# Retention and a swish MLP on one core: where outputs of three chunks lie in PSUM, how the first weights are loaded and used, and the order of the second batch's steps

## The chip, the core and the metric

The kernel runs on one core of one Trainium2 chip. The metric is the device time of one execution in microseconds (us). TensorE is called PE below, VectorE DVE, ScalarE ACT, GpSimd POOL, and SyncE, which issues nearly all transfers, SP. Every engine works through its own list of instructions in a fixed order, and an instruction that waits holds up all that stand behind it on its engine.

## The reference

Inputs are q, k and v of 8 batches, 8 heads, 576 positions and 64 columns, and the weights of an MLP (512 to 2048 and back). All are float32.

```python
scores = scale * np.matmul(q, k.transpose(0, 1, 3, 2))
gamma = 1.0 - 2.0 ** (-5.0 - np.arange(H))
Dmat = np.where(rel >= 0, gamma[:, None, None] ** rel, 0.0)   # rel = row - column
attn = np.matmul(scores * Dmat, v)
x = attn.transpose(0, 2, 1, 3).reshape(B * S, H * D)          # 4608 x 512
h = x @ w_in
out = (h * (1.0 / (1.0 + np.exp(-beta * h)))) @ w_out
```

So there is a causal retention with a decay for each head, and then an MLP with a swish in it. The kernel folds the decay into q and k/v (`gq`, `gv`), so that the mask on the scores is a plain causal one.

## The kernel before

**Attention in chunks.** Of each batch the first 512 positions are four chunks of 128 keys. `seq` lists them: indices 0 to 3 are batch 0, 4 to 7 batch 1, and so on. For index i the steps are: `pre` (POOL casts the keys to `kn` and scales the values to `vn`), `t_k` (four PE transposes into PSUM, ACT copies them to `kT`), `a_sc` (16 PE matmuls make the scores of 8 heads in two PSUM tiles `sc`, DVE multiplies each by the mask into `R`, 128x512 at a time), `a_cross` (4 matmuls with the running state `sbd` of the chunks before), `a_O` (8 matmuls of `R` and `vn` into the output tile `O`), `a_x` (a copy of `O` to `xT`, the input of the MLP, on ACT or DVE), and `a_st` (4 matmuls that add to the state in PSUM, and two ACT copies of it to `sbd`, or to `end` after the last chunk). `t_q` transposes the queries.

**MLP in blocks of 512 rows.** `up(m, fo)` makes one of 16 slices of 128 hidden units: four matmuls over `ko` with 512 columns into a PSUM tile `ph`, and an ACT Silu into `gT`. `down(m, ms, f0)` is four matmuls into `po`; after 16 of them DVE copies `po` to `ot` and SP issues the store. The tiles `ph` and `po`, and some of attention, share the PSUM tag `mm` with three buffers, so a new `ph` waits until the third tile before it has been read. The tags `sc` and `O` have two buffers each; with `st` that makes eight banks. The steps of batch 1 do not all stay with their tag: `a_sc` of an odd index takes its two score tiles from `O`, and `t_k` of indices 6 and 7 transposes into `sc`.

**Order.** The first batch's attention is written out step by step, before any `up`. All that follows is one list `fill` of ups and downs, and `merged` puts further steps into it: each step has a number, and is issued ahead of the first entry of `fill` whose place is not below that number. Place `d0` is the first down of block 0, and `u1 = d0 + 16` the first up of block 1. There are 16 ups before `d0`.

**Weights.** SP loads `w_in` in pieces of columns (four of 256, then two of 512), each with all four `ko`, and behind them `w_out` in four parts of 1 MB, into staging tiles `wt` of 1 MB with four buffers. DVE and POOL cast the pieces to bfloat16 (`cast_w_in`). `cast_w_out` multiplies by 1/beta, three quarters on DVE and one on ACT; its first call stands at `d0 - 4`, so its ACT instruction lies between the Silus of hidden slices 11 and 12.

All of batch 1's loads come behind `w_out` on SP's queue.

Of the kernel before, what the change touches and what calls it, by code (L numbers as in the profile page):

```python
# [19 lines left out]
def kernel(  # L20
# [10 lines left out]
    nc = tc.nc  # L31
    B, H, S, D = q.shape
# [98 lines left out]
    for h in range(H):  # L131
# [16 lines left out]
    causal4 = consts.tile([P, HP, P], BF16, name="causal4")  # L148
    nc.gpsimd.tensor_copy(causal4[:], causal[:].unsqueeze(1).to_broadcast([P, HP, P]))

    causal2 = consts.tile([P, P], BF16, name="causal2")

    NS = 3
# [10 lines left out]
    tiny = consts.tile([P, FO], F32, name="tiny")  # L164
    WG = 4

    pieces = [(f, 256) for f in range(0, 1024, 256)] + [(f, 512) for f in range(1024, d_ff, 512)]
    NP = len(pieces)
    w_in_r = moe_w_in.rearrange("(ko ki) f -> ki ko f", ki=P)
    w_out_r = moe_w_out.rearrange("(fo fi) n -> fi fo n", fi=P)  # L170
# [2 lines left out]
    def load_w_in(g):  # L173
        f0, fn = pieces[g]
        if f0 % 512 == 0:
            whole[0] = stage.tile([P, KO, 512], F32, name="wt", tag="wt", bufs=4)
        t = whole[0][:, :, f0 % 512:f0 % 512 + fn]
        nc.sync.dma_start(t, w_in_r[:, :, f0:f0 + fn])  # L178
        wts[g] = t

    def cast_w_in(g, kos=range(KO)):
        t = wts[g]
        f0, fn = pieces[g]
        for ko in kos:
            on_pool = ko == KO - 1 or g < 4 and ko > 1
            (nc.gpsimd if on_pool else nc.vector).tensor_copy(w_in_sb[:, ko, f0:f0 + fn], t[:, ko])  # L186

    def load_w_out(g):
# [111 lines left out]
    def t_k(i):  # L300
        T = psum.tile([P, HP, P], BF16, name="T", tag="sc" if i in (CB + 2, CB + 3) else "O", bufs=2)
        for p in range(HP):
            nc.tensor.transpose(T[:, p, :], heads(live[i]["kn"], p), ident[:])  # L303
        nc.scalar.copy(live[i]["kT"], T[:])  # L304

    def q_cols(i, r, p):

        b, c = seq[i]
        if b is None:
            return live[i]["qkT"][r, 0, p, :], lambda o: o  # L310
        return (batch[b]["qT"][r, :, p, c * PC:(c + 1) * PC], lambda o: o.rearrange("k (i s) -> k i s", i=CB))

    def a_sc(i):
        L = live[i]
        L["R"] = R = sb.tile([P, 2, HP, P], BF16, name="R", tag="R", bufs=4)

        tag = "mm" if i == CB - 1 else "O" if i >= E and (i - E) % 2 else "sc"
        sc = [psum.tile([P, HP, P], F32, name="sc", tag=tag, bufs=3 if tag == "mm" else 2) for _ in range(2)]
        for p in range(HP):
            for j in range(2):  # L320
                r = slice(j * D, (j + 1) * D)
                rhs, view = q_cols(i, r, p)
                nc.tensor.matmul(view(sc[j][:, p, :]), L["kT"][r, p, :], rhs, start=True, stop=True,  # L323
                                 skip_group_check=True)
        mask = causal if seq[i][0] is not None else causal2
        m_b = mask[:].unsqueeze(1).to_broadcast([P, HP, P])
        if i == CB - 1:

            half = sb.tile([P, HP, P], BF16, name="half", tag="half", bufs=1)
            nc.scalar.copy(half[:], sc[1][:])  # L330
            sc[1] = half
        for j in range(2):
            nc.vector.tensor_tensor(R[:, j], sc[j][:], causal4[:] if i == CB - 1 else m_b, ALU.mult)  # L333

    def a_cross(i, first):

        b, c = seq[i]
        L = live[i]
        if first:
            L["O"] = psum.tile([P, HP, P], F32, name="O", tag="O", bufs=2)  # L340
        if c == 0 and b is not None:
            return
        for p in range(HP):
            rhs, view = q_cols(i, slice(0, P), p)
            if b is None:
                for x in range(2):
                    r = slice(x * TL, (x + 1) * TL)
                    nc.tensor.matmul(L["O"][:, p, r], ends[(2 * c + x) % 4][:, p, :], rhs[:, r],
                                     start=False, stop=True, skip_group_check=True)
            else:  # L350
                nc.tensor.matmul(view(L["O"][:, p, :]), sbds[(c - 1) % NS][:, p, :], rhs,  # L351
                                 start=first and p == 0, stop=not first, skip_group_check=True)

    def a_O(i):

        b, c = seq[i]
        L = live[i]

        early = i < E
        if not early:  # L360
            tag = "sc" if b is not None and b >= QB and c > 1 else "O"
            L["O"] = psum.tile([P, HP, P], F32, name="O", tag=tag, bufs=2)
        O, R, vn = L["O"], L["R"], L["vn"]
        crossed = b is None or c > 0
        for j, p in [(n // HP, n % HP) if early else (n % 2, n // 2) for n in range(H)]:
            nc.tensor.matmul(O[j * D:(j + 1) * D, p, :], vn[:, 2 * p + j, :], R[:, j, p, :],  # L366
                             start=p == 0 and not (early and crossed), stop=early or not crossed,
                             skip_group_check=True)
        if early:
            a_x(i)  # L370

    def a_x(i):
        b, c = seq[i]
        O = live[i]["O"]
        if b is None:
            x = xt(B)[:, :, c, :]
        else:
            x, O = xt(b)[:, :, :, c * PC:(c + 1) * PC], O.rearrange("k p (i s) -> k p i s", i=CB)
        if i == CB - 1:
            nc.vector.tensor_copy(x[:, :2], O[:, :2])  # L380
            nc.scalar.copy(x[:, 2:], O[:, 2:])
        else:
            on_act = i < E or i % 2 == 0 if i < 2 * E else b is not None and c == 1
            (nc.scalar.copy if on_act else nc.vector.tensor_copy)(x, O[:])  # L384
# [21 lines left out]
    def up(m, fo, c0=0, cn=CB):  # L406
        if m not in gts:
            gts[m] = sb.tile([P, FO, CB, P], BF16, name="gT", tag="gT", bufs=2)
        w = slice(c0 * PC, (c0 + cn) * PC)
        ph = psum.tile([P, CB, P], F32, name="ph", tag="mm", bufs=3)  # L410
        ph = ph.rearrange("f i s -> f (i s)")[:, :cn * P].rearrange("f (i s) -> f i s", i=CB)
        for ko in range(KO):
            nc.tensor.matmul(ph, w_in_sb[:, ko, fo * P:(fo + 1) * P], xts[m][:, ko, :, w],  # L413
                             start=(ko == 0), stop=(ko == KO - 1))
        nc.scalar.activation(gts[m][:, fo, :, w], ph, ACT.Silu, scale=beta_sb[:, fo:fo + 1])  # L415
# [37 lines left out]
    def F(f, *a):  # L453
        return lambda: f(*a)
# [26 lines left out]
    pre(3, (0,))  # L481
    a_sc(2)
    t_k(3)
    warm_up(1, 128)
    a_cross(2, True)
    a_sc(3)
    pre(2, (1,))
    a_st(2)
    a_O(2)
    pre(3, (1,))  # L490
    warm_up(2, 128)
    a_cross(3, True)
    a_O(3)
    cast_w_in(0)
    a_st(3)
    cast_w_in(1)
# [4 lines left out]
                            fill=0.0, base=0, channel_multiplier=-1)  # L501
    nc.gpsimd.memset(causal2[:TL, TL:], 0.0)

    fill = [F(up, 0, fo) for fo in range(FO)]
    d0 = len(fill)
    fill += [F(down, 0, ms, f0) for f0 in range(0, FO, 4) for ms in range(3)]
    fill += [F(down, 0, 3, f0) for f0 in range(0, FO, 4)]
# [13 lines left out]
    def second(i):  # L521
        for f in (a_O, lambda j: a_cross(j, False), a_x):
# [98 lines left out]
```

## Time and profile before

| | us |
|---|---|
| median of three runs (311.30 to 312.04) | 311.78 |
| the profiled execution, in all | 311.92 |
| its span, first to last instruction | 310.1 |
| PE busy in the span | 298.5 (96%) |
| ACT busy | 143.0 (46%) |
| DVE busy | 106.9 (34%) |
| POOL busy | 96.0 (31%) |

The profiled execution is 0.14 us above the median, and 1.8 us of it lie outside the span. The granted TensorE clock is 0.998 of full speed over the whole span. A matmul of 512 columns starts 0.216 us after the one before it when nothing waits, one of 256 columns 0.108 us, one of 128 columns 0.056 us; the longer means in the profile's groups (365 ns for the 512 columns) count the pipeline's depth too. Some matmul records are missing from the trace; such a hole looks like an idle PE of 0.2 us with the reason "issue".

### The profile page before, as it was taken

How to read it: one execution, taken by the hardware profiler on the slowest of the kernel's cores; microseconds unless marked ns; L12 is line 12 of the kernel's file. 1: busy time of each engine (PE TensorE's matmuls, PEld its weight loads, DVE VectorE, ACT ScalarE, POOL GpSimd, SP SyncE). 2: the span in 40 equal slices, each digit the busy share in tenths (PEclk: the TensorE clock that was granted, in tenths of full speed). 3: DMA queues.
4: the chain of work that ended last, by engine and by line, in shares of the span. 5: the costliest groups of instructions: out<-in, count | busy, mean ns of one | idle time of the engine just before them, and what ended most of it. 6: DMA issues, size and time to landing. Idle time of an engine off the chain costs nothing.

```text
span 310.1 us, 5363 instructions
## 1 busy us (share of the span) xinstructions
PE 298.5 (96%) x2144; PEld 157.8 (51%) x2177; DVE 106.9 (34%) x191; ACT 143.0 (46%) x256; POOL 96.0 (31%) x131
## 2 busy tenths in 40 slices
PE   7789999999999999999999999999999999999995
PEld 5544456775544454454554545455545444444444
DVE  7554476342531342434430434043405420010012
ACT  5567626995138412560186117711673037207700
POOL 4663026846524282254308031902420000000000
PEclk9999999999999999999999999999999999999999
DMA  8999999998989999999897697968852110031011
GB/s 207 221 355 387 380 232 273 233 257 179 202 197 162 224 189 235 218 212 198 133 234 107 136 205 207 201 115 192 196 76 37 68 70 0 17 88 34 0 70 68
DMA packets 123897, 52.79 MB, mean 170 GB/s; under 512 B 105680, under 2 KB 116320, under 8 KB 123872
## 3 DMA queue, kind: packets, MB, share of 16 engines
q1 hardware_dynamic: 98496, 46.15, 61.5%
q10 hardware_dynamic: 25376, 6.30, 13.6%
q8 instruction: 17, 0.28, 0.4%
q14 instruction: 8, 0.07, 0.1%
HBM read 36.71 MB, written 9.44 MB: 149 GB/s over the span
## 4 chain that ended last, share of the span: by engine, by line
PE 85%; DMA 6%; SPq 5%; DVE 1%; issue 1%; ACT 1%; POOL 1%; POOLq 0%
PE po L426 40%; PE ph L413 35%; DMA wt<-in_moe_w_in_dram 4%; SPq L94 3%; PE O L366 3%; PE sc L323 3%; DMA qn<-in_q_dram 2%; PE O L351 2%; PE st L396 2%; SPq L178 1%; POOL qs L247 1%; PE T L297 1%; PE T L303 1%; ACT gT L415 0%; DVE xT L384 0%
## 5 line engine op out<-in xcount | busy, mean ns | idle before, releaser
L415 ACT ACTIVATE gT<-ph,beta_sb 128x512 bf16<-128x512 f32 (+1 forms) x154 | 99.2, 659 | 86.3 <-PE ph L413 83.4
L413 PE MATMUL ph<-xT,w_in_sb 128*128 128x512 bf16 (+1 forms) x600 | 129.3, 365 | 3.2 <-DVE w_in_sb L186 0.9
L426 PE MATMUL po<-w_out_sb,gT 128*128 128x512 bf16 (+2 forms) x591 | 126.7, 368 | 1.1 <-issue 0.3
L413 PEld LDWEIGHTS <-w_in_sb 128*128 128x128 bf16 x616 | 58.7, 98 | 65.0 <-DVE w_in_sb L186 2.3
L426 PEld LDWEIGHTS <-gT 128*128 128x128 bf16 x608 | 57.1, 98 | 62.5
L333 DVE TENSOR_TENSOR R<-sc,causal 128x512 bf16<-128x512 f32 x71 | 44.3, 684 | 68.9 <-PE sc L323 68.9
L433 DVE COPY ot<-po 128x512 f32<-128x512 f32 (+2 forms) x38 | 25.0, 662 | 92.1 <-PE po L426 92.0
L255 POOL TENSOR_TENSOR vn<-kvn,gv 128x512 bf16<-128x512 f32 x32 | 33.4, 1042 | 22.8 <-DMA kvn<-in_v_dram 11.5
L247 POOL TENSOR_TENSOR qs<-qn,gq 128x512 bf16<-128x512 f32 x24 | 24.3, 1042 | 33.2 <-DMA qn<-in_q_dram 33.2
L273 POOL CAST kn<-kvn 128x512 bf16<-128x512 f32 x32 | 19.6, 612 | 47.7 <-DMA kvn<-in_k_dram 47.3
L401 ACT CAST sbd<-st 64x256 bf16<-64x256 f32 x48 | 17.4, 362 | 15.0 <-PE st L396 14.3
L384 DVE CAST xT<-O 128x512 bf16<-128x512 f32 x24 | 15.8, 688 | 19.6 <-PE O L366 9.6
L384 ACT CAST xT<-O 128x512 bf16<-128x512 f32 x11 | 6.4, 586 | 32.2 <-PE O L351 25.2
L396 PE MATMUL st<-vn,kn 128*128 128x128 bf16 x128 | 12.4, 219 | 0.2 <-POOL vn L255 0.2
L396 PEld LDWEIGHTS <-kn 128*128 128x128 bf16 x128 | 9.3, 98 | 5.0 <-issue 0.2
L366 PE MATMUL O<-R,vn 128*64 128x128 bf16 x288 | 10.7, 221 | 0.0
L323 PE MATMUL sc<-qT,kT 64*128 64x128 bf16 x256 | 10.3, 217 | 0.4 <-ACT kT L304 0.2
L366 PEld LDWEIGHTS <-vn 128*64 128x64 bf16 x288 | 8.5, 110 | 4.1 <-issue 3.6
L323 PEld LDWEIGHTS <-kT 64*128 64x128 bf16 x288 | 8.1, 94 | 3.8 <-ACT kT L304 1.5
L304 ACT COPY kT<-T 128x512 bf16<-128x512 bf16 x12 | 6.9, 586 | 4.8 <-PE T L303 4.8
L208 PE MATMUL ph<-warm 128*128 128x128 f32 (+1 forms) x24 | 7.0, 429 | 1.2 <-DVE warm L119 1.2
L186 DVE CAST w_in_sb<-wt 128x256 bf16<-128x256 f32 (+1 forms) x14 | 6.0, 476 | 5.2 <-DMA wt<-in_moe_w_in_dram 5.2
(56 smaller groups left out, 90.2 us busy)
## 6 DMA issues: line engine op xcount, KB each, us to landing
qn<-in_q_dram SPq DMA_DIRECT2D x16, 512.0 KB, 5.8
kvn<-in_k_dram SPq DMA_DIRECT2D x32, 256.0 KB, 5.9
kvn<-in_v_dram SPq DMA_DIRECT2D x32, 256.0 KB, 5.6
out_dram<-ot SPq DMA_DIRECT2D x31, 256.0 KB, 2.7
wt<-in_moe_w_out_dram SPq DMA_DIRECT2D x4, 1024.0 KB, 9.5
wt<-in_moe_w_in_dram SPq DMA_DIRECT2D x4, 512.0 KB, 7.5
wt<-in_moe_w_in_dram SPq DMA_DIRECT2D x2, 1024.0 KB, 11.8
out_dram<-ot SPq DMA_DIRECT2D x9, 128.0 KB, 2.4
```

The costliest lines, as they stand in the source:

```text
L247: e.tensor_tensor(batch[b]["qs"][:, cs, hs], q_tiles[b][:, hs, cs].rearrange("p h i d -> p i h d"), gq[:, cs, hs].unsqueeze(3).to_broadcas ...
L255: nc.gpsimd.tensor_tensor(live[i]["vn"][:], kv_tiles.pop(i)[:, 1], gains(gv, c), ALU.mult)
L273: nc.gpsimd.tensor_copy(kn[:, c % 2], t[:, 0])
L323: nc.tensor.matmul(view(sc[j][:, p, :]), L["kT"][r, p, :], rhs, start=True, stop=True, skip_group_check=True)
L333: nc.vector.tensor_tensor(R[:, j], sc[j][:], causal4[:] if i == CB - 1 else m_b, ALU.mult)
L366: nc.tensor.matmul(O[j * D:(j + 1) * D, p, :], vn[:, 2 * p + j, :], R[:, j, p, :], start=p == 0 and not (early and crossed), stop=early or ...
L384: (nc.scalar.copy if on_act else nc.vector.tensor_copy)(x, O[:])
L396: nc.tensor.matmul(st[:, p, :], heads(L["kn"], p), heads(L["vn"], p), start=(c == 0 and p == 0), stop=True, skip_group_check=True)
L413: nc.tensor.matmul(ph, w_in_sb[:, ko, fo * P:(fo + 1) * P], xts[m][:, ko, :, w], start=(ko == 0), stop=(ko == KO - 1))
L415: nc.scalar.activation(gts[m][:, fo, :, w], ph, ACT.Silu, scale=beta_sb[:, fo:fo + 1])
L426: nc.tensor.matmul(po[:, :nn], gT[:, fo, ms, :], w_out_sb[:, fo, n0:n0 + nn], start=(fo == 0), stop=(fo == FO - 1))
L433: nc.vector.tensor_copy(ot, po[:, :nn])
```

## The change

It has five parts, which all act in the first 70 us of the program or so.

- The output tiles of indices 3, 5 and 7 are made as two tiles of half the width in two PSUM banks (`split`), and `a_x` copies one on DVE and the other on ACT. Before, index 3 was one bank copied by both engines in turn, and 5 and 7 were one bank copied by DVE.
- The mask of index 3 no longer goes through an ACT copy (`half`) and a widened mask (`causal4`); DVE reads both score tiles from PSUM. The last copies and the third `a_cross` of batch 0 change places with other steps.
- `w_in` is loaded in six pieces of 256 columns and one of 512; the first two are loaded in two halves each, `ko` 0 and 1 and then 2 and 3. `up_pair` makes hidden slices 0 and 1, and then 2 and 3, two at a time: both with `ko` 0 and 1 first, then both with 2 and 3. POOL now casts every second `ko` (`ko` 0 and 1 of the first piece).
- Steps of batch 1 are moved: `t_q` 0 by one place, `t_k` 5 by one, both `a_sc` of indices 4 and 5 by one, `a_st` 4 by one, `t_k` 6 behind `second(4)`, `t_k` 7 by one, and `a_sc` and `a_st` of 6 and 7 by one to two.
- `a_x` of batch 0 becomes a step of its own.

```diff
-    pieces = [(f, 256) for f in range(0, 1024, 256)] + [(f, 512) for f in range(1024, d_ff, 512)]
+    pieces = [(f, 256) for f in range(0, 1536, 256)] + [(f, 512) for f in range(1536, d_ff, 512)]
...
-        nc.sync.dma_start(t, w_in_r[:, :, f0:f0 + fn])
+        for w in (slice(0, 2), slice(2, KO)) if g < 2 else (slice(0, KO),):
+            nc.sync.dma_start(t[:, w], w_in_r[:, w, f0:f0 + fn])
...
-            on_pool = ko == KO - 1 or g < 4 and ko > 1
+            on_pool = ko < 2 if g == 0 else ko % 2
...
-        if i == CB - 1:
-            half = sb.tile([P, HP, P], BF16, name="half", tag="half", bufs=1)
-            nc.scalar.copy(half[:], sc[1][:])
-            sc[1] = half
         for j in range(2):
-            nc.vector.tensor_tensor(R[:, j], sc[j][:], causal4[:] if i == CB - 1 else m_b, ALU.mult)
+            nc.vector.tensor_tensor(R[:, j], sc[j][:], m_b, ALU.mult)
+    def split(i):
+        return i in (CB - 1, CB + 1, 2 * CB - 1)
+    def new_O(i):
+        b, c = seq[i]
+        if split(i):
+            tags = ("sc", "sc") if i == CB - 1 else ("O", "sc")
+            live[i]["O"] = [psum.tile([P, 2, P], F32, name="O", tag=t, bufs=2) for t in tags]
...
+        if split(i):
+            nc.vector.tensor_copy(x[:, :2], view(Os[0]))
+            nc.scalar.copy(x[:, 2:], view(Os[1]))
         else:
-            on_act = i < E or i % 2 == 0 if i < 2 * E else b is not None and c == 1
-            (nc.scalar.copy if on_act else nc.vector.tensor_copy)(x, O[:])
+            on_act = i < 2 * E or b is not None and c == 1
+            (nc.scalar.copy if on_act else nc.vector.tensor_copy)(x, view(Os[0]))
...
+    def up_pair(m, fo, u):
...
+        for f, ko in [(f, ko) for ko in (0, 1) for f in fs] if u == 0 else [(f, ko) for f in fs for ko in (2, 3)]:
+            nc.tensor.matmul(phs[f][:], w_in_sb[:, ko, f * P:(f + 1) * P], xts[m][:, ko],
+                             start=(ko == 0), stop=(ko == KO - 1))
+            if ko == KO - 1:
+                nc.scalar.activation(gts[m][:, f], phs[f][:], ACT.Silu, scale=beta_sb[:, f:f + 1])
...
-    fill = [F(up, 0, fo) for fo in range(FO)]
+    fill = [F(up_pair, 0, fo, u) for fo in (0, 2) for u in range(2)] + [F(up, 0, fo) for fo in range(4, FO)]
...
-               [(d0 + 7, F(pre_q, 1, n)) for n in range(4)] + [(d0 + 10.6, F(t_q, 1, 0)), (d0 + 12.6, F(t_q, 1, 1))],
+               [(d0 + 7, F(pre_q, 1, n)) for n in range(4)] + [(d0 + 11.6, F(t_q, 1, 0)), (d0 + 12.6, F(t_q, 1, 1))],
...
-                (d0 + 12.7, F(t_k, 4)), (d0 + 12.8, F(t_k, 5)), (d0 + 13.8, F(a_sc, 4)), (d0 + 13.81, F(a_sc, 5)),
-                (d0 + 14.8, F(a_st, 4)), (d0 + 15.9, F(second, 4))],
+                (d0 + 12.7, F(t_k, 4)), (d0 + 14, F(t_k, 5)), (d0 + 14.1, F(a_sc, 4)), (d0 + 15, F(a_sc, 5)),
+                (d0 + 15.7, F(a_st, 4)), (d0 + 15.9, F(second, 4))],
...
-                (d0 + 15.8, F(t_k, 6)), (d0 + 15.91, F(t_k, 7)), (u1 + 1.8, F(a_sc, 6)), (u1 + 1.81, F(a_sc, 7)),
-                (u1 + 2.8, F(a_st, 6)), (u1 + 8.8, F(second, 6))]]
+                (d0 + 15.95, F(t_k, 6)), (u1 + 1, F(t_k, 7)), (u1 + 3, F(a_sc, 6)), (u1 + 3.01, F(a_sc, 7)),
+                (u1 + 4, F(a_st, 6)), (u1 + 8.8, F(second, 6))]]
```

More of the change, by code (lines that the diff above doesn't have):

```diff
@@ L147 @@
                             fill=0.0, base=0, channel_multiplier=-1)
-    causal4 = consts.tile([P, HP, P], BF16, name="causal4")
-    nc.gpsimd.tensor_copy(causal4[:], causal[:].unsqueeze(1).to_broadcast([P, HP, P]))
     causal2 = consts.tile([P, P], BF16, name="causal2")
@@ L326, in a_sc, with O_of, opens @@
         m_b = mask[:].unsqueeze(1).to_broadcast([P, HP, P])
-        if i == CB - 1:
-            half = sb.tile([P, HP, P], BF16, name="half", tag="half", bufs=1)
-            nc.scalar.copy(half[:], sc[1][:])
-            sc[1] = half
         for j in range(2):
-            nc.vector.tensor_tensor(R[:, j], sc[j][:], causal4[:] if i == CB - 1 else m_b, ALU.mult)
+            nc.vector.tensor_tensor(R[:, j], sc[j][:], m_b, ALU.mult)
[6 more added lines that the diff above has]
+            live[i]["O"] = [psum.tile([P, 2, P], F32, name="O", tag=t, bufs=2) for t in tags]
+        else:
+            tag = "sc" if b is not None and b >= QB and c > 1 else "O"
+            live[i]["O"] = [psum.tile([P, HP, P], F32, name="O", tag=tag, bufs=2)]
+    def O_of(i, p):
+        Os = live[i]["O"]
+        return Os[p // 2][:, p % 2] if split(i) else Os[0][:, p]
+    def opens(i, p):
+        return p == 0 or split(i) and p == 2
     def a_cross(i, first):
         b, c = seq[i]
-        L = live[i]
         if first:
-            L["O"] = psum.tile([P, HP, P], F32, name="O", tag="O", bufs=2)
+            new_O(i)
         if c == 0 and b is not None:
@@ L344, in a_cross @@
             rhs, view = q_cols(i, slice(0, P), p)
+            O = O_of(i, p)
             if b is None:
@@ L347, in a_cross @@
                     r = slice(x * TL, (x + 1) * TL)
-                    nc.tensor.matmul(L["O"][:, p, r], ends[(2 * c + x) % 4][:, p, :], rhs[:, r],
+                    nc.tensor.matmul(O[:, r], ends[(2 * c + x) % 4][:, p, :], rhs[:, r],
                                      start=False, stop=True, skip_group_check=True)
             else:
-                nc.tensor.matmul(view(L["O"][:, p, :]), sbds[(c - 1) % NS][:, p, :], rhs,
-                                 start=first and p == 0, stop=not first, skip_group_check=True)
+                nc.tensor.matmul(view(O), sbds[(c - 1) % NS][:, p, :], rhs,
+                                 start=first and opens(i, p), stop=not first, skip_group_check=True)
     def a_O(i):
@@ L360, in a_O @@
         if not early:
-            tag = "sc" if b is not None and b >= QB and c > 1 else "O"
-            L["O"] = psum.tile([P, HP, P], F32, name="O", tag=tag, bufs=2)
-        O, R, vn = L["O"], L["R"], L["vn"]
+            new_O(i)
+        R, vn = L["R"], L["vn"]
         crossed = b is None or c > 0
         for j, p in [(n // HP, n % HP) if early else (n % 2, n // 2) for n in range(H)]:
-            nc.tensor.matmul(O[j * D:(j + 1) * D, p, :], vn[:, 2 * p + j, :], R[:, j, p, :],
-                             start=p == 0 and not (early and crossed), stop=early or not crossed,
+            nc.tensor.matmul(O_of(i, p)[j * D:(j + 1) * D], vn[:, 2 * p + j, :], R[:, j, p, :],
+                             start=opens(i, p) and not (early and crossed), stop=early or not crossed,
                              skip_group_check=True)
-        if early:
-            a_x(i)
     def a_x(i):
         b, c = seq[i]
-        O = live[i]["O"]
         if b is None:
-            x = xt(B)[:, :, c, :]
+            x, view = xt(B)[:, :, c, :], lambda o: o
         else:
[L378 to L381, printed above, removed]
-        else:
-            on_act = i < E or i % 2 == 0 if i < 2 * E else b is not None and c == 1
-            (nc.scalar.copy if on_act else nc.vector.tensor_copy)(x, O[:])
+            x, view = xt(b)[:, :, :, c * PC:(c + 1) * PC], lambda o: o.rearrange("k p (i s) -> k p i s", i=CB)
+        Os = live[i]["O"]
+        if split(i):
+            nc.vector.tensor_copy(x[:, :2], view(Os[0]))
+            nc.scalar.copy(x[:, 2:], view(Os[1]))
+        else:
+            on_act = i < 2 * E or b is not None and c == 1
+            (nc.scalar.copy if on_act else nc.vector.tensor_copy)(x, view(Os[0]))
     def a_st(i):
@@ L415, in up @@
         nc.scalar.activation(gts[m][:, fo, :, w], ph, ACT.Silu, scale=beta_sb[:, fo:fo + 1])
+    phs = {}
+    def up_pair(m, fo, u):
+        if m not in gts:
+            gts[m] = sb.tile([P, FO, CB, P], BF16, name="gT", tag="gT", bufs=2)
+        fs = (fo, fo + 1)
+        if u == 0:
+            for f in fs:
+                phs[f] = psum.tile([P, MB], F32, name="ph", tag="mm", bufs=3)
+        for f, ko in [(f, ko) for ko in (0, 1) for f in fs] if u == 0 else [(f, ko) for f in fs for ko in (2, 3)]:
[3 more added lines that the diff above has]
+                nc.scalar.activation(gts[m][:, f], phs[f][:], ACT.Silu, scale=beta_sb[:, f:f + 1])
     pos_, ots = {}, {}
@@ L474 @@
     a_O(0)
+    a_x(0)
     a_sc(1)
@@ L483 @@
     t_k(3)
+    a_x(1)
     warm_up(1, 128)
+    a_sc(3)
     a_cross(2, True)
-    a_sc(3)
     pre(2, (1,))
@@ L489 @@
     a_O(2)
+    a_x(2)
     pre(3, (1,))
@@ L493 @@
     a_O(3)
+    a_x(3)
     cast_w_in(0)
@@ L525, in second @@
         a_st(i + 1)
-    streams = [[(0, F(load_w_out, 0)), (1.1, F(cast_w_in, 2)), (3.1, F(cast_w_in, 3)), (3.2, F(load_w_out, 1)),
-                (6.1, F(cast_w_in, 4)), (6.2, F(load_w_out, 2)), (10.1, F(cast_w_in, 5)), (10.2, F(load_w_out, 3))],
+    streams = [[(0, F(load_w_out, 0)), (0.1, F(cast_w_in, 2)), (2.1, F(cast_w_in, 3)), (2.2, F(load_w_out, 1)),
+                (4.1, F(cast_w_in, 4)), (6.1, F(cast_w_in, 5)), (6.2, F(load_w_out, 2)), (8.1, F(cast_w_in, 6)),
+                (8.2, F(load_w_out, 3))],
                [(d0 - 4 + 3.3 * g, F(cast_w_out, g)) for g in range(WG)],
```

## The prediction

> **What bounds the kernel now.** I read the page first, then a table by stage (cut where the first up starts, at d0, where batch 1's first MLP matmul is near, and after its last attention wait), then PE's waits, and then the order of time in two places.
>
> ```profile
> PE 298.5 (96%) x2144; PEld 157.8 (51%) x2177; DVE 106.9 (34%) x191; ACT 143.0 (46%) x256; POOL 96.0 (31%) x131
> ```
>
> ```profile
> 0.00:19.40 19.40, 14.90 (x149) 10.51 (x149) 12.14 (x34) 11.34 (x23) 10.73 (x28) 1.00 1.09 240
> 19.40:34.10 14.70, 14.00 (x62) 6.19 (x65) 6.98 (x18) 11.39 (x19) 5.24 (x12) 1.00 1.05 382
> 34.10:50.10 16.00, 15.79 (x107) 8.19 (x108) 11.00 (x21) 5.40 (x10) 4.60 (x6) 1.00 1.08 274
> 50.10:60.40 10.30, 9.66 (x130) 7.71 (x129) 4.92 (x8) 8.82 (x22) 7.32 (x8) 1.00 1.09 247
> 60.40:310.10 249.70, 244.18 (x1700) 125.21 (x1727) 71.82 (x113) 106.06 (x187) 68.14 (x79) 1.00 0.68 143
> ```
>
> The columns are the stretch, its length, busy us of PE, PEld, DVE, ACT and POOL, the clock, the DMA share and GB/s. PE is full from 19.4 us on. In the last stretch, most of the missing 5.5 us are lost records (holes of one matmul with the reason "issue"). So a us that PE waits before 60 us is carried to the end, and one that it saves too, if nothing later takes it back. From 19.4 to 34.1 the DMA engines are always busy, at 382 GB/s: the weights arrive as fast as they can.
>
> ```profile
> 26.06 1.51 DVE L186 CAST w_in_sb<-wt 128x512 bf16<-128x512 f32 x3 [2.02 <-DMA wt<-in_moe_w_in_dram]
> ...
> 28.77 1.51 DVE L186 CAST w_in_sb<-wt 128x512 bf16<-128x512 f32 x3 [1.20 <-DMA wt<-in_moe_w_in_dram]
> ...
> 31.53 0.72 ACT L198 ACTIVATE w_out_sb<-wt,rbeta_sb 128x512 bf16<-128x512 f32 x1
> ...
> 32.16 1.98 ACT L415 ACTIVATE gT<-ph,beta_sb 128x512 bf16<-128x512 f32 x3
> ...
> 34.12 0.38 PE L426 MATMUL po<-w_out_sb,gT 128*128 128x512 bf16 x1
> ```
>
> The casts start as the loads land: those shown at 26.04, 28.75 and (w_out) 31.45; the four smaller pieces before them at 18.83, 20.33, 21.83 and 23.32. That is 1.50 us per 512 KB piece, 2.71 per MB. PE starts its first up at 19.48, waits 0.6 us for the 1 MB piece's casts near 27.3, and starts the downs (d0) at 34.12.
>
> **Start.** Index 3's two half copies no longer follow each other (18.59 and 19.05 before), and the ACT copy of the mask (0.58 at 16.49) goes, so the states and x come earlier: the last state copy about 0.4 us, x complete near 18.5 instead of 19.42. The first half piece, half of a 1.50 us landing earlier, is there at about 18.1; the first of POOL's two casts (0.4 each) lets PE begin at 18.55 instead of 19.48. None of this survives, for two reasons.
>
> First, the bytes. Pieces 4 and 5 now have 256 columns, so that their MB takes 2 x 1.50 = 3.00 us instead of 2.71. All later landings are 0.28 later: the last MB of w_in at 29.03, w_out at 31.73. POOL casts ko 1 and 3 of that MB, 0.87 each beside DVE: they are ready at 29.08 + 1.5 to 1.75 = 30.6 to 30.85 (PE alone would ask for ko 3 near 30.1 or before). Then 13 matmuls of 0.216 would put d0 at 33.45 to 33.7.
>
> Second, ACT. Its w_out instruction stands between the Silus of slices 11 and 12 and waits for w_out's landing. Slice 15 needs the PSUM buffer of slice 12. Before, Silu 12 ended at 32.85 and PE wanted the buffer at 33.24: covered by 0.4. Now w_out starts at 31.73 + 0.08, Silu 12 at + 0.63, ends at + 0.69 = 33.13, and slice 15 starts at 33.18, with PE ready at 32.6 to 32.85. Four matmuls later, d0 = 34.04. **The gain at d0 is 0.08 us**, from a head start of 0.9. Bounds: 1.0 if the landings move forward by 0.95, -0.2 if the three more transfers cost 0.1 each. Taken: 0.08, by the landing intervals, the nearest rows.
>
> Landings could move because in the trace's packets one 16,384-byte instruction packet holds a DMA engine from 15.98 for 1.42 us; weights land about 2.1 us after the sum of bytes has reached them before and after it, where the earlier k and v loads land 1.2 us after. So about 0.95 us hangs on which engine it meets, and when.
>
> The Trainium skill ("DMA: Bandwidth & Descriptors", section Bandwidth) speaks against smaller loads: it gives about 2.0 us fixed per DMA and advises a MiB or more. By it three more loads would cost up to 6 us if nothing overlapped. The rows have landings 1.50 us apart for half a MB, so queued loads do not pay it one by one.
>
> **Batch 1.** From d0 PE's list is the same work in another order. Twelve downs of 0.863 end at 44.40. The next down waits 0.04 for DVE's first `ot`, since q lands 0.28 later. With transposes (0.89 + 0.45), two downs, scores (0.66), a down (0.86) and the state (0.22) PE is through at 50.11. Before, the same work and no wait: 34.12 + 16.03 = 50.15.
>
> ```profile
> 48.07 2.48 DVE L333 TENSOR_TENSOR R<-sc,causal 128x512 bf16<-128x512 f32 x4 [0.94 <-PE sc L323]
> ...
> 50.47 0.64 PE L366 MATMUL O<-R,vn 128*64 128x128 bf16 x16
> ...
> 52.22 1.05 PE L413 MATMUL ph<-xT,w_in_sb 128*128 128x256 bf16 x8 [0.34 <-DVE xT L384]
> ...
> 52.53 0.58 ACT L304 COPY kT<-T 128x512 bf16<-128x512 bf16 x1
> ...
> 58.95 0.74 ACT L401 CAST end<-st 64x256 bf16<-64x256 f32 x2
> 59.72 1.72 ACT L415 ACTIVATE gT<-ph,beta_sb 128x256 bf16<-128x256 f32 x4
> ```
>
> (a) The four masks R of indices 4 and 5 start 0.43 after the scores (47.64) and take 2.48. Before, two downs, the state and one transpose lay between scores and O (2.8 us): the masks were just covered. Now one down and the state lie there, 1.64 us from the scores' start at 48.47. O of index 4 needs the tags' buffer that the third mask frees: 48.90 + 1.88 = 50.78, a wait of 0.72; index 5 the fourth, 51.38, a wait of 0.31. Behind them stand cross, state and transpose 6, done at 52.40.
>
> (b) x of index 5 in two halves: DVE 0.42, ACT 0.37 (the half rows of index 3) instead of 0.69. The first up waits 0.13 instead of 0.50: a gain of 0.37.
>
> (c) Transpose 7 now follows the first up, so that on ACT its copy stands behind the x half (52.15 to 52.52), two state copies (to 53.28), kT 6 (53.88) and a Silu (54.26); it ends at 54.75. The second score tile of index 6 takes the `sc` buffer that this copy frees. PE is there at 54.07, after three ups: a wait of 0.73. Queued behind: all ups. Before, that copy ended at 53.1 and no one waited.
>
> (d) The wait of 0.2 for a Silu near 56 stays. x of index 7 in halves removes 0.27 of the 0.29 that PE waited at 59.44. But ACT gets 0.37 more just there: x 6 to 60.18, half of x 7 to 60.47, two end copies to 61.24, Silu 9 to 61.74. The third up after that needs Silu 9's buffer: it starts at 61.79, PE was ready at 61.17, a wait of 0.62. Before, Silu 9 ended at 60.19 and that up started at 60.31, covered by 0.1.
>
> At this up the two lists have done the same work: 61.79 against 60.31, **1.48 later**, the 0.08 of d0 included. Nothing behind is moved, and PE's rows there have no slack to give back.
>
> The skill's "Perfetto Trace Analysis" (Optimizing Scalar/DVE Operations) says that breaking up instructions may finish work sooner where ACT or DVE cause bubbles without being saturated. By it, (b) and (d) alone would gain 0.64. In (d) the rows from 58.47 to 61.4 leave ACT no hole, so the condition fails there.
>
> Sum: 311.92 + 1.48 = 313.40 for the profiled execution, 0.14 less for the median: 313.2. DVE's, POOL's and DMA's later work only gets more cover. An ACT transpose issue of 2.29 us makes PE wait 0.6 at 164 us; a shift may drop or double that, so 0.6 to both sides.
>
> **Rivals.** Faster: the new order makes no new wait. Its place is the masks of 4 and 5, and the copy of kT 7. Then the change keeps the 0.08, 0.37 and 0.27: 311.1. It decides when four masks end within 1.64 us of the scores' start; the row gives 2.91, and it also needs ACT to copy kT 7 by 54.07. Only the short slack speaks for it. Chance 0.10.
>
> Nearly the same: landings 0.95 earlier, since the instruction packet misses the late engine. d0 is 33.1, the batch-1 waits stay: 313.2 - 0.95 = 312.3. For it: the PE list has other places for its fetches. Against: the instructions before it are nearly the same in number. Chance 0.16.
>
> That the change doesn't split or reorder as it says is excluded by the instruction order of the built program: O of 5 and 7 have two copies, and only one down stands between scores and O.
>
> **How the numbers follow.** Main case 0.70 at 313.2, with its bounds 312.6 to 313.9. 0.04 stays for what I don't see, spread over both sides. 0.2% of 311.78 is 0.62, about what a measurement of this kernel can tell. The main case is slower but for its lowest edge, and the second rival at 312.3 lies at the boundary of 312.40: slower 0.75, same 0.14, faster 0.11. The range reaches to the second rival and a little below, 312.0, and to 313.9.
>
> **What would show it.** First up near 18.6; a PE wait near 30.5 for POOL's casts; slice 15 waiting for ACT; d0 at 34.0; PE waiting for R near 50.8 and 51.4, for ACT's kT near 54.8, for a Silu near 61.8. Wrong if d0 is below 33.3, or if PE's waits from 50 to 62 us sum to less than 2 us.

## The result, and the profile after

The changed kernel takes 312.70 us (median of 8 runs, 312.35 to 313.34), the kernel before 311.64 (8 runs, 310.88 to 312.04): a ratio of 1.0041, 95% interval 1.0028 to 1.0054, or 1.3 us slower. Measured again beside three of the experiments, it was 1.0040 (1.0026 to 1.0054). The prediction was 313.2, within 312.0 to 313.9, slower: 1.4 us above the 311.78 from which it counts. The profiled execution took 313.34, the longest of the eight, with a span of 311.6 against 310.1 before.

The page's line of engines, of after:

```profile
PE 299.9 (96%) x2144; PEld 158.6 (51%) x2177; DVE 105.6 (34%) x191; ACT 142.9 (46%) x257; POOL 97.7 (31%) x134
```

PE's share is the same 96% as before, and DVE and ACT have hardly moved: the loss doesn't show in shares. The table by stage, cut as the one of before: at the first up, at d0, at 50.1 us (near batch 1's first MLP matmul) and at the third up after index 7:

```profile
0.00:18.80 18.80, 15.14 (x149) 11.09 (x150) 12.09 (x33) 11.01 (x22) 10.52 (x27) 1.00 1.09 236
18.80:33.90 15.10, 14.38 (x62) 6.18 (x65) 6.42 (x18) 10.71 (x18) 6.95 (x15) 1.00 1.06 374
33.90:50.10 16.20, 15.99 (x107) 8.21 (x107) 10.19 (x20) 5.17 (x8) 4.40 (x6) 1.00 1.08 279
50.10:61.70 11.60, 10.14 (x131) 7.89 (x130) 5.13 (x10) 9.82 (x25) 8.49 (x11) 1.00 1.08 247
61.70:311.60 249.90, 244.21 (x1699) 125.23 (x1727) 71.78 (x113) 106.20 (x187) 67.31 (x77) 1.00 0.68 141
```

The columns are those of the table in the prediction. The start is 0.6 us shorter, the stage of the ups 0.4 longer, and from d0 to the third up after index 7 it is 27.8 us where it was 26.3. The last stage is as long as before within 0.2. PE's waits from the first up on:

```profile
PE ph L422 <- ACT gT L424: 1.6, 3, 1.0
PE O L377 <- DVE R L326: 0.7, 2, 0.6
...
PE sc L321 <- ACT kT L302: 0.3, 1, 0.3
PE ph L437 <- DVE xT L389: 0.3, 1, 0.3
PE ph L437 <- ACT gT L440: 0.2, 1, 0.2
```

The columns are the time in all, the number of waits and the longest. In batch 1 two waits are new by name: PE for DVE's masks (`R`), and for ACT's `kT`. That of batch 1's first up for `xT` is no longer listed. The 1.0 in the first line lies near 166 us and belongs to ACT's transposes. The start in order of time:

```profile
28.97 1.18 DVE L184 CAST w_in_sb<-wt 128x512 bf16<-128x512 f32 x2 [2.02 <-DMA wt<-in_moe_w_in_dram]
29.00 1.62 POOL L184 CAST w_in_sb<-wt 128x512 bf16<-128x512 f32 x2 [1.79 <-DMA wt<-in_moe_w_in_dram]
...
31.74 0.72 ACT L196 ACTIVATE w_out_sb<-wt,rbeta_sb 128x512 bf16<-128x512 f32 x1 [1.32 <-DMA wt<-in_moe_w_out_dram]
...
32.37 2.47 ACT L424 ACTIVATE gT<-ph,beta_sb 128x512 bf16<-128x512 f32 x4
33.09 1.02 PE L422 MATMUL ph<-xT,w_in_sb 128*128 128x512 bf16 x4 [0.30 <-ACT gT L424]
...
33.95 0.81 PE L451 MATMUL po<-w_out_sb,gT 128*128 128x512 bf16 x3
```

This is the chain that the prediction gave: ACT waits 1.32 us for `w_out`, the four last Silus stand behind it, slice 15 (at 33.09) waits for the first of them, and d0 is 33.95 although the first up began at 18.82 instead of 19.48. Then PE's batch 1, and beneath it ACT's part of it:

```profile
48.39 0.62 PE L321 MATMUL sc<-qT,kT 64*128 64x128 bf16 x16
...
50.76 0.41 PE L377 MATMUL O<-R,vn 128*64 128x128 bf16 x8 [0.56 <-DVE R L326]
51.35 0.41 PE L377 MATMUL O<-R,vn 128*64 128x128 bf16 x8 [0.18 <-DVE R L326]
...
54.68 0.38 PE L321 MATMUL sc<-qT,kT 64*128 64x128 bf16 x7 [0.31 <-ACT kT L302]
...
61.68 1.91 PE L422 MATMUL ph<-xT,w_in_sb 128*128 128x256 bf16 x16 [0.32 <-ACT gT L424]
63.42 0.39 PE L295 MATMUL T<-ident,qs 128*128 128x128 bf16 x4
```

```profile
52.13 0.37 ACT L390 CAST xT<-O 128x256 bf16<-128x256 f32 x1 [0.34 <-PE O L363]
52.41 0.76 ACT L410 CAST sbd<-st 64x256 bf16<-64x256 f32 x2
53.20 0.59 ACT L302 COPY kT<-T 128x512 bf16<-128x512 bf16 x1
53.68 0.48 ACT L424 ACTIVATE gT<-ph,beta_sb 128x256 bf16<-128x256 f32 x1
54.05 0.59 ACT L302 COPY kT<-T 128x512 bf16<-128x512 bf16 x1
...
59.63 0.59 ACT L393 CAST xT<-O 128x512 bf16<-128x512 f32 x1 [0.42 <-PE O L363]
60.12 0.38 ACT L390 CAST xT<-O 128x256 bf16<-128x256 f32 x1
60.38 0.75 ACT L410 CAST end<-st 64x256 bf16<-64x256 f32 x2
61.16 1.21 ACT L424 ACTIVATE gT<-ph,beta_sb 128x256 bf16<-128x256 f32 x3
```

The brackets give PE's idle time alone. Counted from start to start, less the usual interval, the part of the last matmul before a wait that nothing overlaps comes on top: 0.72 and 0.35 us for the two `O`, 0.48 for the scores, 0.48 for the up at 61.68. In ACT's rows there is no bracket from 52.41 to the second `kT` copy, nor behind the one at 59.63 up to the Silu at 61.16: PE waits there for the end of a full queue.

**A measure for the experiments.** The first landing of `w_out` differs between executions by up to 0.95 us, also where the loads are the same, and d0 moves with it. So each trace is read in two parts: d0 less that landing, and the stretch from d0 to the first transpose of batch 2's queries (62.07 before, 63.42 after), in which PE has the same work in all kernels. The stretch is 27.96 us before and 29.48 after.

### The profile page after: what moved, and what is told of

It reads as the page before. It is cut to its first block, busy times and chain, and to the rows that moved or that the text cites. A ratio compares the mean times of both kernels' runs of the same rounds, so it can differ in the third digit from the quotient of the medians.

```text
span 311.6 us, 5372 instructions
## 1 busy us (share of the span) xinstructions
PE 299.9 (96%) x2144; PEld 158.6 (51%) x2177; DVE 105.6 (34%) x191; ACT 142.9 (46%) x257; POOL 97.7 (31%) x134
## 4 chain that ended last, share of the span: by engine, by line
PE 82%; DMA 7%; SPq 4%; ACT 2%; DVE 1%; issue 1%; POOL 1%; ACTq 0%; POOLq 0%
PE po L451 40%; PE ph L422 32%; DMA wt<-in_moe_w_out_dram 3%; SPq L94 3%; PE sc L321 3%; PE O L377 3%; DMA qn<-in_q_dram 2%; DMA wt<-in_moe_w_in_dram 2%; PE st L405 2%; PE O L363 2%; ACT gT L424 1%; DVE R L326 1%; SPq L176 1%; POOL qs L245 1%; PE T L295 1%
## 5 line engine op out<-in xcount | busy, mean ns | idle before, releaser
L424 ACT ACTIVATE gT<-ph,beta_sb 128x512 bf16<-128x512 f32 (+1 forms) x150 | 96.3, 659 | 85.1 <-PE ph L422 84.0
L422 PE MATMUL ph<-xT,w_in_sb 128*128 128x512 bf16 (+1 forms) x585 | 126.3, 365 | 2.5 <-ACT gT L424 1.6
L422 PEld LDWEIGHTS <-w_in_sb 128*128 128x128 bf16 x600 | 57.2, 98 | 62.8 <-issue 2.8
L393 DVE CAST xT<-O 128x512 bf16<-128x512 f32 x22 | 14.5, 687 | 16.7 <-PE O L377 9.7
L184 POOL CAST w_in_sb<-wt 128x256 bf16<-128x256 f32 (+1 forms) x14 | 7.1, 531 | 5.8 <-DMA wt<-in_moe_w_in_dram 5.8
```

The costliest lines, as they stand in the source:

```text
L393: (nc.scalar.copy if on_act else nc.vector.tensor_copy)(x, view(Os[0]))
```

## The experiments

Theory: the start gains next to nothing, since ACT's `w_out` instruction carries the landing on to d0; the new order of batch 1 uncovers the four masks and puts `kT` 7 late; the x halves fill ACT's queue. Rivals: the halves alone cost the time (A), the loads do (B), or the waits overlap, so that taking one away lets the next one in.

| run | kernel | us | ratio to before, 95% | d0 less landing | stretch |
|---|---|---|---|---|---|
| e8_after_again | the change, again | 313.40 | 1.0040 (1.0026 to 1.0054) | 2.29 | 29.53 |
| e1_old_order | the change, batch 1's old order | 311.62 | 0.9987 (0.9971 to 1.0004) | 2.29 | 28.22 |
| e2_only_order | before, new order alone | 313.21 | 1.0036 (1.0022 to 1.0050) | 2.66 | 29.47 |
| e11_start_only | before's batch 1, new start | 311.94 | 1.0002 (0.9987 to 1.0017) | 2.29 | 28.02 |
| e10_45_back | the change, 4 and 5 in old order | 312.42 | 1.0025 (1.0006 to 1.0043) | 2.29 | 28.62 |
| e5_states_dve | the change, two state copies on DVE | 311.90 | 1.0005 (0.9992 to 1.0019) | 2.29 | 28.47 |
| e3_no_split57 | the change, x 5 and 7 in one tile | 313.56 | 1.0048 (1.0029 to 1.0066) | 2.30 | 29.94 |
| e4_old_pieces | the change, before's w_in pieces | 313.27 | 1.0037 (1.0022 to 1.0052) | 2.56 | 29.42 |
| e6_w_out_dve | the change, first w_out part on DVE | 313.66 | 1.0048 (1.0031 to 1.0065) | 1.83 | 30.88 |
| e7_old_both | e1 + e5 + e6 | 310.94 | 0.9975 (0.9957 to 0.9994) | 1.84 | 27.83 |
| e9_q_later | e7, half of the query scaling later | 310.49 | 0.9969 (0.9946 to 0.9993) | 1.83 | 27.53 |
| e12_last_piece | e9, before's split of the last casts | 310.68 | 0.9960 (0.9942 to 0.9978) | 1.91 | 27.29 |

The kernel before ran beside each group: 311.94 us for e1 to e4, 311.82 for e5 to e8, 311.69 for e9 to e12.

**The order or the rest.** e1 puts batch 1's numbers back, e2 puts only the new ones into the kernel before, e11 is e1 with x of 5 and 7 copied as before.

```diff
# e1, from the changed kernel (e2 is the reverse, in the kernel before)
-(d0 + 11.6, F(t_q, 1, 0))
+(d0 + 10.6, F(t_q, 1, 0))
-(d0 + 14, F(t_k, 5)), (d0 + 14.1, F(a_sc, 4)), (d0 + 15, F(a_sc, 5)), (d0 + 15.7, F(a_st, 4))
+(d0 + 12.8, F(t_k, 5)), (d0 + 13.8, F(a_sc, 4)), (d0 + 13.81, F(a_sc, 5)), (d0 + 14.8, F(a_st, 4))
-(d0 + 15.95, F(t_k, 6)), (u1 + 1, F(t_k, 7)), (u1 + 3, F(a_sc, 6)), (u1 + 3.01, F(a_sc, 7)), (u1 + 4, F(a_st, 6))
+(d0 + 15.8, F(t_k, 6)), (d0 + 15.91, F(t_k, 7)), (u1 + 1.8, F(a_sc, 6)), (u1 + 1.81, F(a_sc, 7)), (u1 + 2.8, F(a_st, 6))
# e11, besides e1's
-        return i in (CB - 1, CB + 1, 2 * CB - 1)
+        return i == CB - 1
-            on_act = i < 2 * E or b is not None and c == 1
+            on_act = i < E or i % 2 == 0 if i < 2 * E else b is not None and c == 1
```

> The changed kernel with only batch 1's step numbers put back to those of the kernel before; the half outputs, the loads and the pairs of ups stay. Theory (the new order makes the waits of 0.72, 0.35, 0.48 and 0.48 us before 62 us, and the start gives 0.1 to 0.2 us at d0): faster than the changed kernel by 1.2 to 1.7 us and faster than the kernel before by 0.1 to 0.6 us, since index 5's halves also keep their 0.37. The four waits at 49.98, 50.95, 54.15 and 61.09 us are gone from PE's waits. Rival A (the loads or the halves cost the time, the order does not): within 0.4 us of the changed kernel.

> The kernel before with only the new step numbers of batch 1. Theory: the masks wait 0.7 and 0.3 us, and transpose 7's late copy 0.4 to 0.7 us; in all 1.2 to 1.8 us slower than the kernel before, that is as slow as the changed kernel or slower (up to 0.6 us). Rival A (the halves of x on ACT are the loss, the order alone is harmless): within 0.3 us of the kernel before. Rival B (the masks' wait alone survives, the kT 7 wait needs the x half on ACT): 0.9 to 1.1 us slower.

> The changed kernel with batch 1's old order, and indices 5 and 7 in one tile copied by DVE as before: of the change only the start is left (index 3 in two banks, masks, loads, pairs). Theory (the start gives 0.08 to 0.17 us at d0): d0 2.3 us behind the first landing of w_out, d0 to batch 2's first transpose 27.9 to 28.0 us, the time 0 to 0.3 us below the kernel before. Rival B1 (the start is worth the 0.9 us of its earlier first up): 0.7 us or more below. Rival B2 (the smaller loads cost more than the start gives): 0.2 us above or more.

e1 comes out level with or below the kernel before: the order is worth 0.0054 of the time, 1.7 us, by the two ratios, and 1.26 us by the stretch. The masks' waits are gone; the wait for `kT` (0.35) and that at the third up (0.48) stay, so that the expectation of four waits gone was half right. Of PE in order of time in e1:

```profile
51.32 0.64 PE L377 MATMUL O<-R,vn 128*64 128x128 bf16 x16
...
54.08 0.60 PE L321 MATMUL sc<-qT,kT 64*128 64x128 bf16 x15 [0.18 <-ACT kT L302]
...
61.38 1.80 PE L422 MATMUL ph<-xT,w_in_sb 128*128 128x256 bf16 x15 [0.32 <-ACT gT L424]
```

e2 has the loss with nothing else of the change in it: 1.1 us by the ratio, 1.51 by the stretch. The same of e2:

```profile
51.27 0.41 PE L366 MATMUL O<-R,vn 128*64 128x128 bf16 x8 [0.56 <-DVE R L333]
51.86 0.41 PE L366 MATMUL O<-R,vn 128*64 128x128 bf16 x8 [0.18 <-DVE R L333]
...
53.39 0.61 PE L413 MATMUL ph<-xT,w_in_sb 128*128 128x256 bf16 x4 [0.34 <-DVE xT L384]
...
55.03 0.54 PE L323 MATMUL sc<-qT,kT 64*128 64x128 bf16 x8
```

The masks cost what they cost in the changed kernel, the old wait for x of 5 is still there, and only 0.1 us is lost for `kT`. So the wait for `kT` 7 comes from the x half on ACT more than from the order: it is 0.11 us with the new order alone (e2), 0.35 with the halves alone (e1), 0.48 with both. e2's rival B had it that this wait needs the x half; its price of 0.9 to 1.1 fits the ratio, not the stretch (0.24 of which is a wait for the first `ot`, at 45.3). Rival A, that the halves and not the order are the loss, falls. e11 puts the start at nothing: 1.0002, an interval of -0.4 to +0.5 us. What it excludes is rival B1 (0.7 us faster); a loss of 0.2 (B2) lies inside the interval.

**The two halves of the loss.** e10 puts only the steps of the queries and of indices 4 and 5 back (e1's first two pairs of lines). e5 leaves the order and takes work from ACT's queue where PE waits for it:

```diff
# e5, in a_st
-            nc.scalar.copy(s[r, :, j * D:(j + 1) * D], st[r, :, j * D:(j + 1) * D])
+            on_dve = b == 1 and c % 2
+            (nc.vector.tensor_copy if on_dve else nc.scalar.copy)(s[r, :, j * D:(j + 1) * D], st[r, :, j * D:(j + 1) * D])
```

> The changed kernel with only the steps of the queries and of indices 4 and 5 put back (transposes, scores, state); those of 6 and 7 stay late. Theory (the new order's waits are separate: masks 0.72 and 0.35, late transpose 7 0.48): the masks' waits go, the waits of 0.48 at index 6's second score tile and at the third up after index 7 stay; d0 to batch 2's first transpose 28.3 to 28.7 us instead of 29.5, 0.8 to 1.2 us faster than the changed kernel. Rival (what stands behind takes the masks' 1.07 over, as index 6's scores wait longer): under 0.4 us faster.

> The changed kernel with the two state copies after index 5 and after index 7 on DVE instead of ACT. Theory (ACT's queue behind the x halves makes the waits at the second score tile of index 6 and at the third up after index 7): both waits of 0.48 us go or fall below 0.2, the masks' waits of 0.72 and 0.35 stay; 0.6 to 1.0 us faster than the changed kernel, d0 to batch 2's first transpose 28.5 to 28.9 us. Rival (other work stands behind those waits, such as the PSUM buffers of the Silus): 0.3 us or less.

Of e10, PE's waits between 50 and 63 us in order of time; of e5, ACT around `kT` 7, and then PE's waits in that stretch:

```profile
50.91 0.78 PE L377 MATMUL O<-R,vn 128*64 128x128 bf16 x16
...
54.60 0.38 PE L321 MATMUL sc<-qT,kT 64*128 64x128 bf16 x7 [0.31 <-ACT kT L302]
...
61.59 1.58 PE L422 MATMUL ph<-xT,w_in_sb 128*128 128x256 bf16 x13 [0.32 <-ACT gT L424]
```

```profile
52.20 0.37 ACT L390 CAST xT<-O 128x256 bf16<-128x256 f32 x1 [0.34 <-PE O L363]
52.65 0.59 ACT L302 COPY kT<-T 128x512 bf16<-128x512 bf16 x1
53.22 0.47 ACT L425 ACTIVATE gT<-ph,beta_sb 128x256 bf16<-128x256 f32 x1
53.59 0.58 ACT L302 COPY kT<-T 128x512 bf16<-128x512 bf16 x1
```

```profile
50.82 0.41 PE L377 MATMUL O<-R,vn 128*64 128x128 bf16 x8 [0.56 <-DVE R L326]
51.42 0.41 PE L377 MATMUL O<-R,vn 128*64 128x128 bf16 x8 [0.19 <-DVE R L326]
```

They are mirror images. In e10 the masks' waits are gone but for 0.11 us between the two `O` (0.78 for both, 0.64 in e1), and ACT's two stay; in e5, without the two state copies, the second `kT` copy starts 1.39 us after the x half instead of 1.92, ACT's two waits are gone and the masks' stay. The stretch falls by 0.9 in e10 and by 1.0 in e5: the waits (1.07 and 0.96) are separate, and of neither are more than some 0.2 us taken over by what stands behind. The time of e5 is 1.1 us below e8, beside which it ran, by the ratios (1.5 by the medians); 0.6 to 1.0 was expected. That of e10 is only 0.5 below the changed kernel by the ratios (1.0025 against 1.0041), where 0.8 to 1.2 was expected and under 0.4 by the rival; the intervals overlap. The time decides for neither; the stretch of 28.62, within the 28.3 to 28.7 expected, speaks for the theory.

**The halves of x.** e3 keeps two banks for index 3 alone (e11's first pair of lines).

> The changed kernel with index 3 alone in two banks: x of indices 5 and 7 is one tile, copied by DVE. Theory: the first up waits 0.3 to 0.4 us longer, index 7's first up 0.25 longer; the second score tile of index 6 waits 0.3 to 0.4 less and the Silu 9 wait of 0.48 goes: together within 0.4 us of the changed kernel. Rival A (the halves on ACT are the loss): over 0.7 us faster than the changed kernel.

The edit did not do what its expectation says: without `split`, the changed rule for `on_act` gives x of 5 and 7 whole to ACT, not to DVE. PE then waited for ACT's x (0.39 and 0.44) as well as for `kT` and a Silu, and the stretch is 0.46 longer. So by the stretch halving is better than all of x on ACT (the times are alike, 1.0048 against 1.0041); what it was meant to tell apart stays untested by it. e1 against e11 is that test in the old order: by the stretch the halves lose 0.20 (28.22 against 28.02), by the times they gain (0.9987 against 1.0002) with overlapping intervals. PE's waits say where the 0.20 comes from: the halves save 0.67 at the first ups that read x of 5 and 7 (0.50 to 0.13 and 0.29 to nothing, e11 to e1), and pay 0.83 in the two waits behind ACT (0.35 and 0.48). By the times it is not settled. That the halves earn nothing that these runs resolve while the states stay on ACT is all that can be said.

**The start.** e4 loads the last 1024 columns of `w_in` as two pieces of 1 MB again. e6 takes the ACT instruction out of the first `w_out` part.

```diff
# e4 (and the casts' numbers for one piece less)
-    pieces = [(f, 256) for f in range(0, 1536, 256)] + [(f, 512) for f in range(1536, d_ff, 512)]
+    pieces = [(f, 256) for f in range(0, 1024, 256)] + [(f, 512) for f in range(1024, d_ff, 512)]
# e6, in cast_w_out
-            if i == KO - 1:
+            if i == KO - 1 and g:
```

> The changed kernel with w_in pieces 4 and 5 again as one load of 512 columns. Theory (the two smaller loads delay every later landing by 0.28 us, and ACT's w_out instruction carries that to slice 15 and d0): w_out lands about 31.4 instead of 31.66, the first down starts 0.2 to 0.3 us earlier, and the time is 0.2 to 0.3 us below the changed kernel. Rival C (the landing of w_out does not set d0): the first down within 0.1 us of the changed kernel's and the time within 0.15 us. Rival D (PE runs dry before the 1 MB piece's casts by more than it gains): 0.2 us slower or more.

> The changed kernel with the one ACT instruction of the first w_out part on DVE, so that no Silu of block 0 stands behind w_out's landing. Theory: the wait of 0.46 us before slice 15 goes, d0 is 0.3 to 0.5 us earlier against the first w_out landing (1.8 to 2.0 us after it instead of 2.3), and the time falls by 0.2 to 0.5 us. Rival (something later takes it back: the queries' landing, the first output copy on DVE): d0 earlier but d0 to batch 2's first transpose longer by as much, time within 0.15 us of the changed kernel.

e4's time is that of the changed kernel (1.0037), and in its profiled execution all weights landed late (`w_out` at 32.31). Within the trace the 0.28 us is there all the same: counted from the landing of the whole first piece, `w_out` lands 12.64 us later in e4, 12.62 in before and 12.95 in after. But PE loses it again, with a wait of 0.65 us at 27 us for the 1 MB piece: from the same landing to d0 it is 15.20 us in e4, 15.24 in after and 15.29 in before. So the smaller pieces cost a landing 0.3 us, as predicted, and nothing at d0: there the two sizes are alike. e6 bears the theory and its rival out at once. d0 follows the landing after 1.83 us in place of 2.29, to the 0.46 of the wait that was removed. But PE comes earlier to the next thing, DVE's first output copy, and the rival's queue takes the gain:

```profile
42.48 1.29 DVE L245 TENSOR_TENSOR qs<-qn,gq 128x512 bf16<-128x512 f32 x2 [0.23 <-DMA qn<-in_q_dram]
44.02 1.29 DVE L245 TENSOR_TENSOR qs<-qn,gq 128x512 bf16<-128x512 f32 x2 [0.25 <-DMA qn<-in_q_dram]
45.23 1.88 DVE L458 COPY ot<-po 128x512 f32<-128x512 f32 x3
```

```profile
45.97 0.81 PE L451 MATMUL po<-w_out_sb,gT 128*128 128x512 bf16 x3 [0.90 <-DVE ot L458]
```

DVE's scaling of the queries waits for their landing, `ot` stands behind it, and PE waits 1.06 us for a PSUM buffer. In this execution the last part of `w_out` and the queries also landed about 1.0 us late, which made it worse; the time is 1.0048 against 1.0040 for e8, no difference. A transfer's landing had only moved from one cover to the next.

**The causes together.** e7 is e1 with e5's and e6's edits. e9 also moves the scaling of heads 4 to 7, which only the second query transpose needs, behind the first `ot`. e12 gives DVE three of the last piece's four casts, as in the kernel before.

```diff
# e9, besides e7's
-[(d0 + 7, F(pre_q, 1, n)) for n in range(4)]
+[(d0 + 7 + n // 2 * 2.5, F(pre_q, 1, n)) for n in range(4)]
# e12, besides e9's
-            on_pool = ko < 2 if g == 0 else ko % 2
+            on_pool = ko < 2 if g == 0 else ko == KO - 1 if g == NP - 1 else ko % 2
```

> The changed kernel with batch 1's old step numbers, the state copies after indices 5 and 7 on DVE, and the first w_out part all on DVE. If the three causes add (new order 1.3 to 1.5, ACT's queue 0.6 to 0.9, w_out's ACT instruction 0.2 to 0.5): 2.1 to 2.9 us below the changed kernel and 0.9 to 1.6 us below the kernel before (ratio 0.995 to 0.997). If they overlap (old order alone already has transpose 7's copy out of the way), 0.5 to 0.9 us below the kernel before.

> The kernel of the run before last with old order, states on DVE and w_out's first part on DVE, and now the second half of batch 1's query scaling behind the first output copy on DVE. Theory (DVE's query scaling waits for a landing and holds back the first output copy, which holds back PE by 0.54 us at 44.5): that wait goes below 0.1, d0 to batch 2's first transpose is 27.2 to 27.5 us instead of 27.83, and the time falls by 0.3 to 0.6 us, to 0.995 to 0.997 of the kernel before. Rival (the transposes of the queries then wait themselves for the scaling): within 0.15 us of that run.

> The kernel of the first run of this call, with DVE taking three of the four casts of the last w_in piece, as in the kernel before. Theory (POOL's second cast of 0.87 us is what PE waits for at 30 to 31 us): the three waits there of 0.23 to 0.25 us shrink to 0.1 to 0.3 in all, d0 comes 0.3 to 0.5 us earlier against the landing of w_out, and the time falls by up to 0.4 us. Rival (batch 1's queries land too late for that): d0 earlier, but the steps from d0 on longer by as much.

(The kernel named in e9's expectation is e7, the one in e12's is e9.) By the ratios e7 is 2.0 us below e8 and 0.8 below the kernel before: under the 2.1 to 2.9 of causes that add, and within the 0.5 to 0.9 of causes that overlap. Of what it lacks, 0.54 us is PE's wait for `ot`; the old order also had less of the wait for `kT` 7 to lose (0.35 in e1). e9 removes that wait: the stretch falls to 27.53, 0.03 longer than the expectation's upper end, since 0.22 of it comes back at the second transpose of the queries; its time has moved by no more than the intervals allow. Of e12, the only row of PE from d0 to batch 2's end that has a wait in brackets:

```profile
55.15 1.47 PE L423 MATMUL ph<-xT,w_in_sb 128*128 128x256 bf16 x12 [0.17 <-ACT gT L425]
```

e12's waits at 30 us shrink from 0.50 in e9 to 0.37, counted from start to start, and d0 is not nearer to the landing of `w_out` (1.91), where 0.3 to 0.5 was expected: PE now waits for DVE's casts there, and the rest before d0 is its own work. e9 and e12 beat both kernels, by 1.0 us (0.2 to 1.7) and 1.2 us (0.7 to 1.8) against the kernel before; between the two nothing can be told. Their stretch is 0.4 and 0.7 below that of before.

## Why the prediction was right, step by step

- **d0.** Predicted 34.04 in place of 34.12, measured 33.95, by the chain named. In seven executions of kernels with ACT's instruction and the new loads, d0 comes 2.29 or 2.30 us after the landing, wherever that was between 31.66 and 32.61; e6 takes the chain away and d0 moves by its price. e11 agrees with a gain of 0.08 in time, as it would with a small loss. That the landings were to be 0.28 later for the smaller pieces comes out as 0.32, counted from the first piece's landing (12.95 against 12.62). From there to d0 it is 15.29 us in before and 15.30 in e2, and 15.22 to 15.24 in six of the seven (15.40 in e1, where one piece landed 0.3 late): free of the landings' spread, the gain at d0 is some 0.06 us where 0.08 was predicted.
- **First up.** Predicted 18.55, measured 18.82: in this execution not the weights but x came last, complete at 18.68 where 18.5 was said. The first half piece was there at 16.75 in this execution, 1.35 us before the predicted 18.1, and at 18.0 to 19.0 in all others (in e1, e4 and e10 its first cast came last, and the first up began at 19.26 to 19.48). Neither mattered at d0. The pairs of ups added a wait of 0.35 us at 20.55 for a PSUM buffer that the prediction did not have; it too ended before ACT's chain.
- **(a) Masks.** 0.72 and 0.31 predicted, 0.72 and 0.35 measured; e2 and e5 repeat them, e10 removes them.
- **(b) x of 5.** A wait of 0.13 predicted, 0.12 measured.
- **(c) `kT` 7.** ACT's queue is the one named, and e5 removes the wait by taking work out of it. But the prediction put the wait down to the step's move, and e1 and e2 put 0.35 of it down to the x half and only 0.11 to the move by itself. The size is off as well: 0.73 predicted, 0.48 measured. The copy ended at 54.63 instead of 54.75, and PE came to the scores at 54.15 instead of 54.07; the rest is the start interval of the first score matmul. This term was 0.25 too large.
- **(d) x of 7.** The wait before the first up vanished; the third up after it waited 0.48, not 0.62, and e5 shows that the state copies in front of the Silu make it.
- **Sum at that up.** 61.79 predicted, 61.68 measured, 1.37 later than before where 1.48 was said. That it came so near is in part luck: from d0 on the prediction's waits add up to 2.75 us and measure 2.40, and the rest of PE's time, taken as 25.00, measures 25.33 (25.07 before). Two errors of a third of a us cancel; why the rest is 0.26 longer than before was not tested. The sign of being wrong, waits of under 2 us from 50 to 62 us, did not come, counted as the prediction counts them; the brackets alone sum to 1.46.
- **Nothing later gives it back.** True of PE's order, and the 0.6 us at the ACT transposes was a fair bound: that wait is 1.15 us in the trace of after, 0.77 in that of before, 0.29 in e8, which is the same kernel as after. It is noise of one execution, and hides a few tenths in each comparison of spans. So the 313.40 that was predicted for the profiled execution and the 313.34 measured agree better than the method can; the median of 312.70 lies 0.5 below the predicted one, and the ratio gives 1.3 us (0.9 to 1.7) for the predicted 1.4.
- **The rivals.** The masks were not covered, so the faster case fell. The landings did not come earlier: the first four pieces landed 0.1 earlier than before, all later ones 0.2 later. The instruction packet that was blamed for the late engine is there in all traces, at 15.4 to 16.7 us. What the prediction read of it holds in the trace of after too: loads that land by 16.75 do so 0.8 to 1.2 us after the sum of bytes has reached them, those from 18.71 on 2.0 to 2.1 us after. But that the packet sets the landings was argued and has not been shown; no run moves it.

On the Trainium skill's "DMA: Bandwidth & Descriptors": its fixed cost of about 2.0 us per DMA stands in the section "Anatomy of one DMA — SWDGE (gpsimd) path", for DMAs that GpSimd issues, and not in section Bandwidth, which has the advice of a MiB. Here SP issues the loads. After the first half piece, the 256 KB halves landed at 18.71, 19.47 and 20.21, 0.75 apart, and e11 with all three added loads is within 0.5 us of the kernel before. Queued behind each other, these loads did not pay it. Its "Perfetto Trace Analysis" (Optimizing Scalar/DVE Operations) says that breaking up instructions may allow work to be completed sooner where Scalar or Vector aren't saturated but cause bubbles on other engines. ACT is 46% busy over the span and yet had no hole in the two places; taking other work from it there gained 1.1 us (e5), while halving x in the old order gained nothing that these runs resolve (e1 against e11).

## What to carry to other kernels

Before moving a step in a hand-written order, count what stands between each producer and its consumer on PE and compare it with the other engine's whole batch (here four masks, 2.48 us, against 1.64 us of cover), not with the mean of one instruction. An engine at 46% can be the bound for one microsecond: read its rows for brackets at the place, and move away the work that no one there waits for. And a gain at a landing is only kept if the next queue with a landing in it, here DVE's query scaling ahead of the output copy, is moved as well.

## What was not expected of the hardware

- The same queued loads land up to 0.95 us apart from execution to execution (first `w_out` part at 31.66 to 32.61 with the new loads; 31.66 to 32.42 among e9 to e12, which ran as one group), at an unchanged clock of 0.998 to 1.000, and PE's start of the downs follows one for one. A kernel that waits for loads can't be judged to half a microsecond from the span of one trace.
- PE's waits behind ACT's transpose issues, far from any edit, went from 0.29 to 1.15 us near 165 us in two executions of the same kernel.
